# Nine planner constants of a fused attention and feed-forward kernel become a table with sixteen rows

## The chip, the cores and the metric

The kernel runs on one core of a Trainium2 chip. Its time is the device time of one execution in microseconds (us), and lower is better. In the profile the engines have these names: PE is TensorE (matrix products), PEld its loads of weights, DVE is VectorE, ACT is ScalarE, POOL is GpSimd, and SP issues DMA transfers.

## What is computed

One transformer block with adaptive layer norm, for one sequence of 2048 tokens of width 512, in bfloat16:

```python
mod = (silu(c) @ w_mod).reshape(1, 6, 1, 512)
sa, ca, ga, sb, cb, gb = mod[:, 0], ..., mod[:, 5]
h = layernorm(x) * (1 + ca) + sa
x = x + ga * attention(h, wqkv, wo)              # 32 heads of 16
h = layernorm(x) * (1 + cb) + sb
x = x + gb * ((gelu(h @ w_gate) * (h @ w_up)) @ w_down)   # 1792 wide
```

The attention makes 32 x 2048 x 2048 scores and takes the exponential of each of them.

## The kernel before

**Banks and positions.** Scores are made in PSUM, a bank at a time: 128 keys on the partitions and 512 columns, which are 512 queries, or fewer queries and several tiles of keys. All scores together are 2048 such banks, and the kernel puts them into one list, `seq`; the index of a bank in it is its position, `pos`. The queries are cut into seven sets (`SETS`: 512, 512, 256, 256, 256, 128 and 128 tokens). A set takes as many banks as it has tokens, so `ends`, the position at which each set ends, is 512, 1024, 1280, 1536, 1792 and so on. Four neighbouring banks (four heads, the same keys) form a round. The first two units of work, 128 banks, come interleaved; `nsplit` is the position after them.

**Two ways to an exponential.** The score banks of PSUM (`ps_sc`) are six, used as two groups of three (`CH` is 3). Most banks go through ACT: one `ACTIVATE` with the exponential for the two or three banks of a group, written to the ring `E`. Some rounds are done by DVE instead (`new_quad` opens one): for each of the round's four banks one `TENSOR_SCALAR` (`bits`) writes a 16-bit number to `mreg`, `dreg` or `wreg`, and then three operations over 2048 columns (`power_task`: `mant`, `square`, `expo`) make two tiles whose value products PE adds up. A group then has two banks for ACT and one for DVE, or, in the branch of `ALONE`, only banks for DVE. PE multiplies the exponentials by the values into `ps_pv` (`pv_do`); `unit_end` divides by the sum.

**Side work.** Projections, the second layer norm, the output projection and the feed-forward network of the sets that are done run between the scores, piece by piece (`next_side`, `advance`), mostly in the bank `ps_mi`. `plan` gives each of them a start and a due position; `credit` counts the columns of side work that should have been done by now. DVE's work for them and for the rounds lies in `self.tasks`, from which `step` takes it.

**Who sets the order.** The whole order of all engines is fixed while the kernel is built. `rec` notes each operation with what it waits for. `model` keeps a clock for each engine (`self.free`) by formulas for the length of an operation (`cost`), such as, for ACT and DVE,

```python
            return n * 0.833 + (57 if ps else 92)
...
        return n * 1.042 / f + 68
```

with `n` the elements of a partition and `f` a factor for 16-bit operands outside of PSUM. `probe` asks when an operation could begin. The loop in `stream` takes at every turn the time `t` at which PE is free and chooses greedily: the next group of scores, a value product, a piece of side work, or a filler (a product with the identity or with zeros whose result is not used). A filler is put in where PE would wait and the columns of its last 3413 ns, which `short` counts, are below `FILL`; a column counts at full weight for a product over the whole array and at a quarter for one over a part of it. `model` counts a column of PE at 1/2.4 ns throughout. After the loop, `tail` finishes the last two sets with constants of its own (a literal `t + 30` among them), and `prologue`, which lies ahead of the loop, is written out by hand.

**The nine constants.** Each of them is one number for the whole loop before:

- `t + 30` (ready): what can begin within 30 ns counts as ready now.
- `HOLE` 200: the gap in ns on DVE ahead of a bank of scores into which another step is put.
- `BACK` 8: no new round for DVE while this many of its steps wait.
- `FILL` 4200: the columns, as above.
- `credit > 1536` (lag): the credit from which side work goes ahead of scores and value products.
- `+ 500` (early): by how many ns DVE may be busy beyond ACT and still get a bank of the next group.
- `ALONE` 2500: how many ns ACT must be busy ahead for a group to go to DVE alone.
- `AHEAD` 24: how many positions ahead of `pos` a round for DVE must lie, from `nsplit` on.
- `SIDE2` 2500: the credit above which side work gets a second bank, the sixth of the score banks. It is asked only where `pos >= TWO_AT(ends)`, which is `ends[4]`, 1792.

No bank goes to DVE before `("k", 3, 0)`, the last keys of the first heads, is there.

Of the kernel before, what the change touches and what calls it, by code (L numbers as in the profile page):

```python
# [1 line left out]

# [20 lines left out]
NKT = S_TOK // P  # L23
VW = DH + 1
EPS = 1e-5
FILL = 4200


SETS = ((0, 512), (512, 512), (1024, 256), (1280, 256), (1536, 256), (1792, 128), (1920, 128))
# [4 lines left out]
CH = 3  # L34
# [4 lines left out]
CREDIT = 5000  # L39
LATE_AT = lambda ends: ends[4]  # L40
TWO_AT = lambda ends: ends[4]
HOLE = 200
SIDE2 = 2500
ALONE = 2500
AHEAD = 24
NEAR = 8
FIRST = 0
LAST = 3
# [1 line left out]
DUE = lambda ends: (ends[1] + 30, 1420, 1605, ends[4] + 10, ends[5] - 20)  # L50
URGENT = 9
LATE = 2
BACK = 8
END = (0, None)


# [7 lines left out]

COMPUTE = ("pe", "act", "dve", "pool")
ALLENG = ("sp",) + COMPUTE


class _Op:
# [362 lines left out]
class _Kernel(_Recorder):  # L432
# [714 lines left out]
    def short(self, t):  # L1147

        w = 0
        for s, k in reversed(self.log):  # L1150
            if s < t - 3413:
                break
            w += k
        return FILL - w

    def stream(self):
        self.split = True
# [10 lines left out]
        rounds = []  # L1168
        rof = {}
        ends = [0] * len(SETS)  # L1170
# [12 lines left out]
        nsplit = len(seq)  # L1183
# [8 lines left out]
        pos = c = e = rp = loaded = 0  # L1192
# [11 lines left out]
        cand = [k for k, (u, r, g0) in enumerate(rounds) if FIRST <= r < NKT * u[3] // 512 - LAST]  # L1204
# [17 lines left out]

        def new_quad(hot):
            nonlocal quad
            while cand and rounds[cand[0]][2] < pos + (AHEAD if pos >= nsplit else NEAR):
                cand.pop(0)
            if hot or not cand or len(self.spare()) < 2 or pos >= LATE_AT(ends) and self.credit >= CREDIT:
                return False
            rnd = rounds[cand[0]]
            (_, qd, _, W), r, a = rnd  # L1230
            if (a >= pos + 96 or self.backlog() >= BACK or ("v", r * (512 // W) // 4, qd // 2) not in self.have
                    or any(k not in self.have for k in self.keys(seq[a]))):
                return False
            cand.pop(0)
            quad = {"rnd": rnd, "j": [0, 1, 2, 3], "todo": 4, "k": self.spare()[0], "ready": [], "n": 2, "slot": None}
            self.held.add(quad["k"])
            left[rnd[0]] += 1
            self.plain[rnd[0]] -= 1
            vec.update(range(a, a + 4))
            return True  # L1240

        def bits(q, j, k, fill=False):
            kq = self.bufs[q["k"]][0]
            f = lambda: self.ts("dve", kq[:, 512 * j:512 * j + 512].bitcast(U16), self.scp[:, k, :],
                                128 / OCT, BITS_C, ALU.mult, ALU.add)
            if fill and self.free["dve"] + HOLE < self.probe(f):
                self.step("dve", self.free["dve"], 650)
            f()
            q["todo"] -= 1
# [27 lines left out]
        def pv_next():  # L1277

            res = []
            for k in open_rounds():  # L1280
                rnd = rounds[k]
                u, r, g0 = rnd
                if group[u] != cg or any(g0 + j not in self.slot for j in range(4)) or len(res) == 2:
                    break
                if left[u] == 1 and self.blocked(u):
                    break
                src = [self.slot[g0 + j] for j in range(4)]
                if ("v", r * (512 // u[3]) // 4, u[1] // 2) not in self.have:
                    if tq is not None:
                        break  # L1290
                    x = 0.0
                else:
                    x = self.probe(lambda: pv(rnd, 0, src))
                if res:
                    x = max(x, res[0][0])
                res.append((x, 0, k, rnd, 0, src, None))
                if left[u] <= 2:
                    break
            n = 0
            for q in wait:  # L1300
                u = q["rnd"][0]
                if group[u] != cg:
                    break
                for i, src in q["ready"]:
                    if n == 2 or (left[u] == 1 and self.blocked(u)) or (res and left[u] <= 2):
                        break
                    n += 1
                    res.append((self.probe(lambda: pv(q["rnd"], i, src)), 1, i, q["rnd"], i, src, q))
            res.sort(key=lambda x: (max(x[0], t + 30), x[1]))
            return res  # L1310

        def pv_do(x):
# [37 lines left out]

        early, late = self.weight_parts()
        while cg <= group[units[-1]]:
            parts = early or late
            if parts and pos >= loaded and (pos >= ends[FLOW - 1] + 8 if early else ("ffn", FLOW - 1) in self.have):
                parts.pop(0)()
# [3 lines left out]
            t = max(self.pe_now(), virt)  # L1359
# [2 lines left out]

            tq = None
            if c % 2:
                self.two = self.fifth or (pos >= TWO_AT(ends) and self.credit > SIDE2)
            mem, after = take(CH - 1 if (left[units[1]] or self.two) and c % 2 else CH)
            s0 = CH * (c % 2)
            if mem:
                e0 = 0 if e + len(mem) > NSL else e
                if all(owner.get(e0 + i, -1) < rp for i in range(len(mem))):  # L1370
                    tq = self.probe(lambda: self.mm(self.scp[:, s0:s0 + len(mem), 0:P], *filler))
            if tq is not None and tq <= t + 30:
                slack = self.free["act"] - 600 - t
                w = self.next_side()
                if w is not None and pos >= w[1] and self.credit > 1536 and slack > 213 and self.probe(w[4][1]) <= t:
                    self.advance()
                    continue
                if slack > 213 and self.short(t) > 0:
                    self.mm(self.scp[:, s0, :], *filler)
                    continue  # L1380
                if self.free["act"] > t + ALONE and self.free["dve"] < t + 900 and ("k", 3, 0) in self.have:
                    alone = []
                    while len(alone) < CH:
                        if quad is None and not new_quad(overdue()):
                            break
                        alone.append((quad, quad["j"].pop(0)))
                        if not quad["j"]:
                            quad = None
                    if alone:
                        items = [(q["rnd"][2] + j, s0 + i) for i, (q, j) in enumerate(alone)]  # L1390
                        self.require(sorted({k for m, _ in items for k in self.keys(seq[m])}))
                        self.qk([(seq[m], k) for m, k in items])
                        for (q, j), (_, k) in zip(alone, items):
                            bits(q, j, k)
                            close(q)
                        gain(len(items))
                        continue
                g = None
                if len(mem) == CH and ("k", 3, 0) in self.have and self.free["dve"] < max(t + 400, self.free["act"]) + 500:
                    hot = overdue()  # L1400
                    if quad is not None:
                        if not hot - {quad["rnd"][0]}:
                            g = pick(quad)
                    elif new_quad(hot):
                        mem, after = take(CH)
                        g = pick(quad)
                if g is not None:
                    mem, after = take(CH - 1)
# [5 lines left out]
                n = len(mem)  # L1414
# [13 lines left out]
                pos, e, c = after, e0 + n, c + 1  # L1428
                continue
            gap = 1e9 if tq is None else tq - t  # L1430
            tp = pv_next()
            ok = [x[0] <= t + 30 for x in tp[:2]] + [False, False]
            w = self.next_side()
            ts = None
            side = False
            if w is not None and pos >= w[1]:
                ts = self.probe(w[4][1])
                n = w[4][0]
                side = (ts <= t + 30 and (self.credit >= n / 2 or (self.short(t) > 0 and self.credit > -2048))
                        and n / 2.4 <= gap + max(0, self.free["act"] - 600 - t - max(0, gap)))  # L1440
            if ok[0] and (ok[1] or self.pe_mode == 2 or tq is None or not mem) and not (
                    side and self.credit > 1536 and (tq is not None or not mem or self.free["act"] > t + 1200)):
                pv_do(tp[0])
                continue
            if side:
# [2 lines left out]
            if ok[0] and gap > 400:  # L1448
                pv_do(tp[0])
                continue  # L1450
            nxt = [x for x in [tq, ts] + [x[0] for x in tp] if x is not None and x > t + 30]
            if self.tasks:
                nxt.append(max(self.free["dve"], t + 100))
            nxt = min(nxt) if nxt else t + 100
            if gap > 213 and self.short(nxt) > 0:
                fill = next((f for f in fillers() if self.probe(f) <= t + 30), None)
                if fill is not None:
                    fill()
                    continue
# [264 lines left out]
```

## Time and profile before

| what | before |
|---|---|
| median of 3 runs | 834.76 us (834.16 to 834.98) |
| the profiled execution | 833.36 us |
| its span, first to last instruction | 831.6 us |
| ACT busy | 797.4 us, 96% |
| PE busy | 760.6 us, 91% |
| DVE busy | 746.7 us, 90% |
| POOL busy | 4.7 us, 1% |
| DMA | 43.74 MB, mean 53 GB/s |

The profile is of one execution; the times come from other runs. Busy time is the time in which an engine has an instruction at work. The chain that ended last is followed back from the last instruction, at each step to what released it. In the rows of groups stand the line of the program, engine, operation, what is written and read, how often; then busy us, mean ns of one, and the idle time just before them with its releaser. The lines are those of helpers that record all operations: L339 is ACT's, L321 PE's, L343, L351, L356 and L360 are DVE's. A wait "A <- B" is time in which A had to wait for B: us in total, times, the longest. A row of a stretch gives its length, then each engine's busy us with the number of instructions, the granted TensorE clock (1.00 is full speed), the share of the DMA engines and GB/s.

### The profile page before, as it was taken

What the parts mean: (1) busy time and instruction counts of PE and PEld (TensorE: products, weight loads), DVE (VectorE), ACT (ScalarE), POOL (GpSimd) and SP (SyncE); (2) the same over time, 40 slices, a digit from 0 to 9 for tenths busy, and PEclk for the clock granted to TensorE, in tenths of its full rate; (3) what the DMA queues carried; (4) which work ended last, traced back from release to release, by engine and by line L of the source; (5) the groups of instructions that cost most, each with busy time, mean ns of one, the idle gap of its engine ahead of it and who ended that gap; (6) DMA issues with size and microseconds to landing.
All of it is one profiled execution on the core that took longest, in us unless ns stands there. A gap on an engine that the chain in (4) does not pass through costs nothing.

```text
span 831.6 us, 30174 instructions
## 1 busy us (share of the span) xinstructions
PE 760.6 (91%) x13685; PEld 297.1 (36%) x13690; DVE 746.7 (90%) x1335; ACT 797.4 (96%) x743; POOL 4.7 (1%) x13
## 2 busy tenths in 40 slices
PE   7999998989999988899899989999999999999998
PEld 3333332322222222222233333333543344345556
DVE  7857999989999999999899999979999999599874
ACT  6999999999999999999999999999999999999982
POOL 2000000000000000000000000000000000000000
PEclk9999999999999999999999999999999999999999
DMA  8010000000003111110003222112462432500000
GB/s 294 37 28 10 10 10 9 10 9 9 9 5 108 47 46 34 47 34 22 22 8 97 60 60 55 40 29 78 129 173 59 123 99 72 158 11 11 18 9 14
DMA packets 76362, 43.74 MB, mean 53 GB/s; under 512 B 20557, under 2 KB 74634, under 8 KB 76234
## 3 DMA queue, kind: packets, MB, share of 16 engines
q1 hardware_dynamic: 76232, 41.82, 18.0%
q8 instruction: 107, 1.75, 0.9%
q14 instruction: 21, 0.17, 0.1%
q10 hardware_dynamic: 2, 0.00, 0.0%
HBM read 39.18 MB, written 2.61 MB: 50 GB/s over the span
## 4 chain that ended last, share of the span: by engine, by line
ACT 77%; PE 13%; DVE 4%; DMA 3%; SPq 2%; issue 1%; DVEq 0%
ACT E L339 73%; PE ps_sc L321 6%; PE ps_mi L321 5%; ACT hreg L339 3%; SPq L389 2%; ACT L339 2%; PE ps_pv L321 1%; DMA rb<-scr_rec 1%; DVE mreg L351 1%; DMA den<-scr_den 1%; DMA mreg<-in_w_mod_dram 1%; DVE mreg L343 1%; DVE dreg L351 0%; DVE wreg L343 0%; DMA scr_den<-osb 0%
## 5 line engine op out<-in xcount | busy, mean ns | idle before, releaser
L339 ACT ACTIVATE E<-ps_sc 128x1024 bf16<-128x1024 f32 (+1 forms) x705 | 752.9, 1292 | 19.7 <-PE ps_sc L321 19.3
L321 PE MATMUL ps_sc<-qT,kme 32*128 32x256 bf16 (+2 forms) x1600 | 193.2, 304 | 24.3 <-ACT E L339 21.4
L321 PE MATMUL ps_sc<-qT,kmo 32*128 32x256 bf16 (+2 forms) x1664 | 193.2, 298 | 22.3 <-ACT E L339 18.9
L351 DVE TENSOR_SCALAR mreg<-ps_sc 128x512 uint16<-128x512 f32 x256 | 171.9, 685 | 19.6 <-PE ps_sc L321 17.1
L321 PE MATMUL ps_pv<-E,vaug 128*17 128x256 bf16 (+2 forms) x2548 | 150.4, 300 | 1.6 <-DVE osb L360 0.9
L321 PE MATMUL ps_mi<-wreg,mreg 128*32 128x256 bf16 (+1 forms) x1888 | 106.7, 326 | 5.4 <-DVE hreg L343 2.4
L351 DVE TENSOR_SCALAR dreg<-ps_sc 128x512 uint16<-128x512 f32 x148 | 99.9, 685 | 9.5 <-PE ps_sc L321 8.6
L321 PEld LDWEIGHTS ps_sc<-qT,kme 32*128 32x128 bf16 x1600 | 53.3, 92 | 144.1 <-ACT E L339 121.7
L321 PEld LDWEIGHTS ps_sc<-qT,kmo 32*128 32x128 bf16 x1664 | 54.9, 92 | 134.5 <-ACT E L339 117.3
L321 PEld LDWEIGHTS ps_pv<-E,vaug 128*17 128x17 bf16 x2548 | 51.2, 89 | 57.0 <-issue 40.7
L351 DVE TENSOR_SCALAR mreg<-mreg 128x2048 uint16<-128x2048 uint16 x103 | 69.8, 682 | 0.3
L321 PEld LDWEIGHTS ps_mi<-wreg,mreg 128*32 128x32 bf16 x1888 | 41.1, 95 | 46.9 <-issue 18.8
L321 PE MATMUL ps_pv<-mreg,vaug 128*17 128x256 bf16 (+2 forms) x840 | 47.5, 295 | 2.0 <-DVE mreg L343 0.7
L343 DVE TENSOR_TENSOR mreg<-mreg 128x2048 bf16<-128x2048 bf16 x39 | 47.4, 1215 | 0.1
L321 PE MATMUL ps_mi<-hreg,wreg 128*32 128x512 bf16 x480 | 40.3, 385 | 0.6 <-DVE vaug L360 0.5
L321 PE MATMUL ps_mi<-xs,ident 128*32 128x512 bf16 (+1 forms) x432 | 35.0, 380 | 0.1
L321 PE MATMUL ps_mi<-wo,onorm 128*32 128x512 bf16 x416 | 33.7, 384 | 0.5 <-DVE xs L343 0.4
L351 DVE TENSOR_SCALAR dreg<-dreg 128x2048 uint16<-128x2048 uint16 x49 | 33.5, 684 | 0.0
L343 DVE TENSOR_TENSOR hreg<-ps_mi,hreg 128x512 bf16<-128x512 f32 x47 | 32.2, 684 | 1.1 <-PE ps_mi L321 0.7
L360 DVE CAST hreg<-ps_mi 128x512 bf16<-128x512 f32 x46 | 31.5, 685 | 1.7 <-PE ps_mi L321 1.0
L321 PE MATMUL ps_pv<-dreg,vaug 128*17 128x256 bf16 (+2 forms) x464 | 29.1, 303 | 2.1 <-DVE dreg L343 1.3
L343 DVE TENSOR_TENSOR dreg<-mreg,dreg 128x2048 bf16<-128x2048 bf16 x25 | 30.3, 1212 | 0.1
(166 smaller groups left out, 696.4 us busy)
## 6 DMA issues: line engine op xcount, KB each, us to landing
mreg<-in_B_w_up_dram SPq DMA_DIRECT2D x32, 256.0 KB, 2.9
mreg<-in_B_w_gate_dram SPq DMA_DIRECT2D x28, 256.0 KB, 3.5
mreg<-in_B_w_down_dram SPq DMA_DIRECT2D x16, 256.0 KB, 2.8
dreg<-in_B_w_down_dram SPq DMA_DIRECT2D x12, 256.0 KB, 4.8
mreg<-in_w_mod_dram SPq DMA_DIRECT2D x1, 2048.0 KB, 12.8
rb<-scr_rec SPq DMA_DIRECT2D x64, 32.0 KB, 1.8
out_dram<-xs SPq DMA_DIRECT2D x16, 128.0 KB, 2.0
rb<-scr_rec SPq DMA_DIRECT2D x116, 16.0 KB, 1.8
```

The source lines that it names most:

```text
L321: return self.rec("pe", lambda e: e.matmul(out, lhsT, rhs, start=start, stop=stop, tile_position=tp), [lhsT, rhs, *after], [out], cost=(n, ...
L339: return self.rec("act", lambda e: e.activation(out, in_, func, scale=scale, **kw), rd, wr, cost=self.cost("act", out, [in_], "act") + load)
L343: return self.rec(eng, lambda e: e.tensor_tensor(out, a, b, op), [a, b], [out], cost=self.cost(eng, out, [a, b], "tt"))
L351: return self.rec(eng, lambda e: e.tensor_scalar(out, a, s1, s2, **kw), rd, [out], cost=self.cost(eng, out, [a], "ts") + (60 if len(rd) > ...
L360: return self.rec(eng, lambda e: e.tensor_copy(out, in_), [in_], [out], cost=self.cost(eng, out, [in_], "ts"))
L389: return e.dma_start(out, in_)
```

## The change

The five named constants and the four literals become fields of a row of `RULES`. `stream` sets `self.rule` at every turn of its loop by the position, one row for each 128 banks. The rows differ from one another; they were chosen by a hill climb on the time that `model` gives. Nothing else is changed: the operations, their formulas, `plan` with its due positions, `prologue` and `tail` are as before. In the cut diff below, the places where a constant is replaced by the field of the same meaning are shown once each.

```diff
-FILL = 4200
...
-HOLE = 200
-SIDE2 = 2500
-ALONE = 2500
-AHEAD = 24
...
-BACK = 8
+RULES = (
+    (5, 100, 6, 4200, 1024, 400, 3200, 32, 1024),
+    (30, 200, 8, 3600, 1536, 500, 2500, 24, 2500),
+    (30, 200, 8, 4200, 1536, 500, 3200, 28, 2500),
+    (30, 300, 8, 4200, 1536, 400, 1900, 24, 2500),
+    (80, 200, 8, 3600, 2048, 500, 2500, 24, 1800),
+    (15, 200, 8, 4200, 2048, 500, 1900, 24, 3200),
+    (80, 300, 10, 3600, 1536, 650, 2500, 24, 1024),
+    (60, 200, 8, 4200, 1536, 500, 1900, 24, 3200),
+    (30, 200, 8, 4200, 1536, 500, 2500, 24, 3200),
+    (15, 200, 10, 3000, 1536, 500, 2500, 24, 2500),
+    (30, 200, 8, 4200, 1536, 400, 3200, 28, 1024),
+    (30, 200, 8, 4200, 1536, 850, 1900, 32, 1024),
+    (30, 450, 6, 3300, 1536, 500, 1900, 24, 3200),
+    (80, 200, 8, 4200, 2048, 850, 3200, 32, 3200),
+    (30, 300, 10, 4200, 1536, 500, 3200, 28, 2500),
+    (60, 200, 7, 3900, 1536, 850, 2500, 24, 3200),
+)
...
+_Rule = collections.namedtuple("_Rule", "ready hole back fill lag early alone ahead side2")
...
-        return FILL - w
+        return self.rule.fill - w
...
-            while cand and rounds[cand[0]][2] < pos + (AHEAD if pos >= nsplit else NEAR):
+            while cand and rounds[cand[0]][2] < pos + (self.rule.ahead if pos >= nsplit else NEAR):
...
-            if (a >= pos + 96 or self.backlog() >= BACK or ("v", r * (512 // W) // 4, qd // 2) not in self.have
+            if (a >= pos + 96 or self.backlog() >= self.rule.back or ("v", r * (512 // W) // 4, qd // 2) not in self.have
...
-            if fill and self.free["dve"] + HOLE < self.probe(f):
+            if fill and self.free["dve"] + self.rule.hole < self.probe(f):
...
-            res.sort(key=lambda x: (max(x[0], t + 30), x[1]))
+            res.sort(key=lambda x: (max(x[0], t + self.rule.ready), x[1]))
...
         while cg <= group[units[-1]]:
+            self.rule = _Rule(*RULES[min(pos // 128, len(RULES) - 1)])
...
-                self.two = self.fifth or (pos >= TWO_AT(ends) and self.credit > SIDE2)
+                self.two = self.fifth or (pos >= TWO_AT(ends) and self.credit > self.rule.side2)
...
-                if w is not None and pos >= w[1] and self.credit > 1536 and slack > 213 and self.probe(w[4][1]) <= t:
+                if w is not None and pos >= w[1] and self.credit > self.rule.lag and slack > 213 and self.probe(w[4][1]) <= t:
...
-                if self.free["act"] > t + ALONE and self.free["dve"] < t + 900 and ("k", 3, 0) in self.have:
+                if self.free["act"] > t + self.rule.alone and self.free["dve"] < t + 900 and ("k", 3, 0) in self.have:
...
-                if len(mem) == CH and ("k", 3, 0) in self.have and self.free["dve"] < max(t + 400, self.free["act"]) + 500:
+                if len(mem) == CH and ("k", 3, 0) in self.have and self.free["dve"] < max(t + 400, self.free["act"]) + self.rule.early:
```

More of the change, by code (lines that the diff above doesn't have):

```diff
@@ L1 @@
+import collections
 import numpy as np
@@ L1371, in stream @@
                     tq = self.probe(lambda: self.mm(self.scp[:, s0:s0 + len(mem), 0:P], *filler))
-            if tq is not None and tq <= t + 30:
+            if tq is not None and tq <= t + self.rule.ready:
                 slack = self.free["act"] - 600 - t
                 w = self.next_side()
-                if w is not None and pos >= w[1] and self.credit > 1536 and slack > 213 and self.probe(w[4][1]) <= t:
+                if w is not None and pos >= w[1] and self.credit > self.rule.lag and slack > 213 and self.probe(w[4][1]) <= t:
                     self.advance()
@@ L1431, in stream @@
             tp = pv_next()
-            ok = [x[0] <= t + 30 for x in tp[:2]] + [False, False]
+            ok = [x[0] <= t + self.rule.ready for x in tp[:2]] + [False, False]
             w = self.next_side()
@@ L1438, in stream @@
                 n = w[4][0]
-                side = (ts <= t + 30 and (self.credit >= n / 2 or (self.short(t) > 0 and self.credit > -2048))
+                side = (ts <= t + self.rule.ready and (self.credit >= n / 2 or (self.short(t) > 0 and self.credit > -2048))
                         and n / 2.4 <= gap + max(0, self.free["act"] - 600 - t - max(0, gap)))
             if ok[0] and (ok[1] or self.pe_mode == 2 or tq is None or not mem) and not (
-                    side and self.credit > 1536 and (tq is not None or not mem or self.free["act"] > t + 1200)):
+                    side and self.credit > self.rule.lag and (tq is not None or not mem or self.free["act"] > t + 1200)):
                 pv_do(tp[0])
@@ L1450, in stream @@
                 continue
-            nxt = [x for x in [tq, ts] + [x[0] for x in tp] if x is not None and x > t + 30]
+            nxt = [x for x in [tq, ts] + [x[0] for x in tp] if x is not None and x > t + self.rule.ready]
             if self.tasks:
@@ L1455, in stream @@
             if gap > 213 and self.short(nxt) > 0:
-                fill = next((f for f in fillers() if self.probe(f) <= t + 30), None)
+                fill = next((f for f in fillers() if self.probe(f) <= t + self.rule.ready), None)
                 if fill is not None:
```

## The prediction

> **What bounds the kernel now.** I read the first part of the profile's page, then the chain that ended last, then the busy time by stretches, and then the waits.
>
> ```profile
> span 831.6 us, 30174 instructions
> PE 760.6 (91%) x13685; PEld 297.1 (36%) x13690; DVE 746.7 (90%) x1335; ACT 797.4 (96%) x743; POOL 4.7 (1%) x13
> ACT 77%; PE 13%; DVE 4%; DMA 3%; SPq 2%; issue 1%; DVEq 0%
> ```
>
> ACT is busy for 797.4 of 831.6 us and holds 77% of the chain. So 34.2 us of the span are not ACT work. The busy time by stretches shows where they lie:
>
> ```profile
> core 0: us, PE busy (x) PEld busy (x) DVE busy (x) ACT busy (x) POOL busy (x), PEclk, DMA share, GB/s
> 0.00:26.00 26.00, 20.81 (x265) 9.40 (x265) 18.66 (x63) 18.10 (x24) 4.34 (x12) 1.00 0.79 264
> 26.00:78.00 52.00, 47.97 (x868) 17.75 (x860) 36.56 (x87) 51.34 (x48) 0.31 (x1) 1.00 0.05 13
> 78.00:390.00 312.00, 283.02 (x3935) 84.14 (x3935) 301.37 (x482) 311.53 (x288) 0.00 (x0) 1.00 0.10 27
> 390.00:702.00 312.00, 289.74 (x5929) 119.19 (x5926) 294.46 (x518) 309.14 (x278) 0.00 (x0) 1.00 0.27 74
> 702.00:728.00 26.00, 24.31 (x493) 9.60 (x490) 15.53 (x27) 25.77 (x26) 0.00 (x0) 1.00 0.45 127
> 728.00:806.00 78.00, 73.34 (x1966) 40.76 (x1963) 66.80 (x133) 75.28 (x72) 0.00 (x0) 1.00 0.06 13
> 806.00:831.60 25.60, 21.45 (x264) 16.29 (x266) 13.32 (x30) 6.25 (x13) 0.00 (x0) 0.98 0.04 12
> ```
>
> The head (to 26) leaves ACT idle 7.9 us and the tail (from 806) 19.35 us. Between them, in 780 us, ACT is idle for 0.66 + 0.47 + 2.86 + 0.23 + 2.72 = 6.9 us only. There the time is how much work ACT is given. DVE is not full there: from 78 to 806 its idle time is 10.63 + 17.54 + 10.47 + 11.20 = 49.8 us. DVE also does softmax banks, so what the planner moves from ACT to DVE is what can shorten the middle. The waits of these two engines: the first row is ACT's from 26 to 806 us, the second DVE's from 78 to 702, the last two DVE's from 702 to 806 (us in total, times, the longest).
>
> ```profile
> ACT E L339 <- PE ps_sc L321: 6.3, 10, 1.2
> DVE mreg L351 <- PE ps_sc L321: 12.1, 24, 2.3
> DVE dreg L351 <- PE ps_sc L321: 5.7, 9, 2.9
> DVE mreg L351 <- PE ps_sc L321: 4.6, 3, 3.0
> ```
>
> ACT's 6.3 us end on PE's scores. DVE waits for the same thing: it has nothing left but a bank of scores that PE hasn't made, since PE waits for ACT to free a buffer. That is a matter of how early the planner gives DVE its next bank.
>
> **What one moved round is worth.** A round of four banks that DVE takes over leaves ACT, mostly as four groups of three that become groups of two.
>
> ```profile
> L339 ACT ACTIVATE E<-ps_sc 128x1024 bf16<-128x1024 f32 x447 | 441.0, 1146 | 5.9 <-PE ps_sc L321 5.5
> L339 ACT ACTIVATE E<-ps_sc 128x1536 bf16<-128x1536 f32 x250 | 364.4, 1576 | 1.5 <-PE ps_sc L321 1.4
> L351 DVE TENSOR_SCALAR mreg<-ps_sc 128x512 uint16<-128x512 f32 x256 | 171.9, 685 | 19.6 <-PE ps_sc L321 17.1
> L351 DVE TENSOR_SCALAR dreg<-ps_sc 128x512 uint16<-128x512 f32 x148 | 99.9, 685 | 9.5 <-PE ps_sc L321 8.6
> ```
>
> ACT gains 1576 - 1146 = 430 ns a bank, 1.72 us a round. Today 256 + 148 = 404 banks, 101 rounds, go by DVE. A round costs DVE four bank operations and three over the whole round (two bit operations and a multiplication). Their means overlap with their neighbours, so I take the pitch from start to start in a full piece of the timeline:
>
> ```profile
> 202.21 0.69 DVE L351 TENSOR_SCALAR mreg<-mreg 128x2048 uint16<-128x2048 uint16 x1
> 202.81 0.68 DVE L351 TENSOR_SCALAR dreg<-dreg 128x2048 uint16<-128x2048 uint16 x1
> 203.42 0.68 DVE L351 TENSOR_SCALAR mreg<-ps_sc 128x512 uint16<-128x512 f32 x1
> 204.02 1.21 DVE L343 TENSOR_TENSOR mreg<-mreg 128x2048 bf16<-128x2048 bf16 x1
> 205.15 1.28 DVE L351 TENSOR_SCALAR dreg<-ps_sc 128x512 uint16<-128x512 f32 x2
> ```
>
> Six at 0.60 and one at 1.13 make 4.73 us. The round also adds one more set of value products on PE; their cover is PE's wait for ACT (below). If the middle gets shorter by 1.72 us, DVE's idle time falls by that too: each round uses 4.73 + 1.72 = 6.45 us of idle DVE. All 49.8 us would hold 7.7 rounds, 13.3 us: that and ACT's 6.9 us are the ceiling, 20.2 us, of what an order can bring in the middle.
>
> **How far the build's clock can be trusted.** The rows of the table were picked by that clock, so what they bring here hangs on it. It is a sum of formulas in the code, and the trace has the same operations. For ACT it is 0.833 ns an element and 57: 910 ns for two banks, 1336 for three. With the counts above (and the six of one bank at 484) that makes 406.8 + 334.0 + 2.9 = 743.7 us; the trace has
>
> ```profile
> L339 ACT ACTIVATE E<-ps_sc 128x1024 bf16<-128x1024 f32 (+1 forms) x705 | 752.9, 1292 | 19.7 <-PE ps_sc L321 19.3
> ```
>
> 9.2 us more, 13 ns on each. For a bank on DVE it has 512 x 1.042 + 68 = 601 ns, and the pitch above is 0.60. So the clock is 1.2% short on ACT, evenly, and right on DVE. And how many banks each engine gets is fixed at the build: a bank that has moved stays moved, however the waits fall.
>
> **The change, part by part.** No operation of the mathematics is added; constants become rows, one for 128 positions. The 2048 positions run from about 14 us (row below) to 806: a row of the table is some 49 us. 63 of the 144 entries differ from before. Eleven of them can't act: side2 is asked only from position 1792, so it is without effect in rows 0 to 13 (ten entries), and ahead only after position 128 (row 0). Row 8 therefore plans by the old rule.
>
> - early, alone, back, ahead, hole decide when DVE is given a bank. They move both ways: early is 650 or 850 in four rows and 400 in three, alone 1900 in five and 3200 in five, back 10 in three and 6 or 7 in three. That looks like a fit of each stretch, and no general opening. I take half of the ceiling: 24.9 us of idle DVE, 3.9 rounds, 6.6 us. The ends are none (0) and all (13.3). The piece from 702 to 728, where DVE does only 15.53 of 26 us, belongs to row 14 and is where I look first.
> - ready and lag move side work and value products against the scores. Their worth is ACT's wait of 6.9 us in the middle; a quarter, 1.6 us, as the wait is in few places (10 stops). Ends: all of it, and as much again lost.
> - fill (3000 to 3900 in six rows) takes out filler products. The worth is nothing, by these rows:
>
> ```profile
> PEld ps_sc L321 <- ACT E L339: 244.3, 569, 1.2
> L321 PE MATMUL ps_mi<-xs,nil x116: 379/379/390, 135.2 to 728.3; 128*32 128x512 bf16 x116
> ```
>
> PE waits 244.3 us for ACT to free score banks, and that wait covers the fillers; without the cover each would cost up to its 0.38 us.
>
> - side2 in row 15 (3200) gives side work a second bank less often, so some groups stay at three banks. From the rows above, 752.9 less 1650 banks at 0.430 leaves 43.4 us for 703 groups, 0.06 us each: ten groups are 0.6 us, counted as nothing.
>
> Head and tail stay. The chain's first exponentials start at 14.37 us, and what lies before is written out by hand; from 806 us the tail's own loop keeps its constants.
>
> ```profile
> 14.37 26.32 ACT E L339 x23
> PEld ps_mi L321 <- DVE hreg L343: 9.6, 25, 1.0
> ```
>
> Sum: 6.6 + 1.6 = 8.2 us. The profiled execution (span 831.6, 833.36 in all) would come to 825.2; it lies 1.4 below the median of the runs, so for the median 834.76 - 8.2 = 826.5 us.
>
> **Rivals.**
>
> Lost in DVE's lateness: the extra rounds go in, but DVE at 301.37 of 312 us is nearly full, and its copies of sums and projections come later; PE, and then ACT, wait for them. The second row of the last fence is such a wait, 9.6 us in 25 places. If it grows by half, all of that falls on ACT and nothing is won on ACT's own wait, the time is 834.76 - 6.6 + 4.8 = 833.0. Against it: the formula for a bank on DVE fits its pitch, so the plan sees this lateness coming.
>
> The order nearly fills DVE: three quarters of both terms, 10.0 + 5.2 = 15.2, so 819.6.
>
> Slower: the TensorE clock. The filler products go in where PE's recent columns fall below fill, and the build's clock counts a column at 1/2.4 ns always: it has no throttle in it. With fill at 3000 to 3600 in rows 1, 4, 6, 9 and 12, PE may fall below what holds its clock. Rows for it:
>
> ```profile
> 611.90:615.30 3.40, 2.21 (x54) 0.83 (x42) 3.10 (x5) 2.86 (x3) 0.00 (x0) 1.00 0.62 161
> 724.60:728.00 3.40, 2.47 (x52) 0.88 (x44) 2.99 (x6) 3.40 (x5) 0.00 (x0) 1.00 0.11 25
> 827.00:830.40 3.40, 0.73 (x4) 0.12 (x2) 2.14 (x4) 0.00 (x0) 0.00 (x0) 0.99 0.17 57
> 806.00:832.00 26.00, 21.45 (x264) 16.29 (x266) 13.32 (x30) 6.25 (x13) 0.00 (x0) 0.97 0.03 11
> ```
>
> PE kept clock 1.00 through pieces with 2.21 and 2.47 busy of 3.40 us. It lost it only after the piece with 0.73: the mean of the last 26 us is 0.97, which is a loss of 0.8 in the last 1.6 us, about half the clock. The first two pieces bear against the rival: each is as long as the stretch over which the code counts columns (3413 ns), and PE was idle for a third of it without losing clock. One piece at half the clock costs between 2 x 2.21 - 3.40 = 1.0 and (at the middle's 283.02 of 312, 3.08 us) 2.8 us, say 1.9. Five such pieces eat 8.2 us; the five rows hold 5 x 49 / 3.4 = 72. With eight, 15.2 us: 826.5 + 15.2 = about 842.
>
> The Trainium skill (TensorE: Matmul & The Clock Gate, "A second HAM failure mode: psum-queue depth-cycling") tells of this way to lose: a PE that micro-idles between groups while it cycles through PSUM banks swings between half and full clock, without any long gap. By that, thinner filling alone would decide, and the time would be the 842 above. This trace disagrees so far: PE waits 569 times for ACT, up to 1.2 us, and the clock stays at 1.00 in every stretch to 806 us.
>
> That the table does nothing would be the old order, within 1 us of 834.76; 52 acting entries speak against it, and I count it with the first rival.
>
> **How the numbers follow.** A measurement of this kernel tells about 0.2%, 1.7 us, from no change. Forecast (gains of 3.5 to 13): 0.73. Nearly full DVE: 0.06. Lost in lateness or without effect: 0.12, of which 0.05 still gain over 1.7 us, 0.05 lie within it and 0.02 beyond it on the other side. Slower by the clock: 0.09. So faster 0.73 + 0.06 + 0.05 = 0.84, same 0.05, slower 0.11. The range takes in the fuller DVE's 819.6 and goes to a gain of nearly nothing, past the lateness's 833.0: 819.5 to 834.5. What lies outside, 842 above all, has about 0.15.
>
> **What would show it.** Right: more than 404 banks by DVE, some 415 to 425; ACT busy lower by 6 to 7 us from 797.4 while its idle time stays at 32 to 34; DVE idle from 78 us to the tail at 20 to 30 us in place of 49.8, most gained between 696 and 750; clock 1.00 to the tail. Wrong: the same 404 banks and a shorter time, which would mean that waits went and not work; ACT waiting for PE or DVE in the middle above 10 us; a clock below 1.00 in rows 1, 4, 6, 9 or 12, which would make the table a loss; a tail from 806 us that is shorter by more than 2 us, as nothing here moves it.

## The result, and the profile after

The changed kernel takes 827.62 us (median of 6 runs, 826.18 to 828.68) against 834.87 us of the kernel before in the same comparison: ratio 0.9904, 95% interval 0.9883 to 0.9924, so some 8 us faster (7.3 by the medians). The profiled execution took 826.18 us.

The first part of its page and the chain's shares:

```profile
span 824.5 us, 29810 instructions
PE 750.5 (91%) x13502; PEld 293.0 (36%) x13502; DVE 750.9 (91%) x1342; ACT 794.4 (96%) x742; POOL 4.6 (1%) x13
ACT 88%; PE 6%; DVE 3%; DMA 2%; issue 0%; SPq 0%; DVEq 0%
```

The span is 7.1 us shorter. Of that, 3.0 us are less ACT work (797.4 to 794.4), and 4.1 us are less ACT idle time (34.2 to 30.1). The chain runs through ACT for 88% in place of 77%. The busy time by stretches, cut as before but with the tail from 800 us on:

```profile
core 0: us, PE busy (x) PEld busy (x) DVE busy (x) ACT busy (x) POOL busy (x), PEclk, DMA share, GB/s
0.00:26.00 26.00, 21.35 (x254) 9.46 (x258) 18.66 (x63) 17.55 (x23) 4.32 (x12) 1.00 0.80 264
26.00:78.00 52.00, 47.76 (x865) 17.84 (x861) 36.43 (x86) 51.34 (x48) 0.31 (x1) 1.00 0.05 12
78.00:390.00 312.00, 281.41 (x3912) 83.62 (x3911) 302.04 (x483) 311.53 (x288) 0.00 (x0) 1.00 0.11 27
390.00:702.00 312.00, 287.13 (x5863) 118.28 (x5866) 297.68 (x525) 310.44 (x282) 0.00 (x0) 1.00 0.27 74
702.00:728.00 26.00, 25.34 (x498) 9.88 (x498) 22.65 (x42) 26.00 (x26) 0.00 (x0) 1.00 0.46 127
728.00:800.00 72.00, 66.97 (x1880) 38.37 (x1875) 61.70 (x121) 71.84 (x69) 0.00 (x0) 1.00 0.06 14
800.00:824.50 24.50, 20.58 (x257) 15.57 (x254) 11.69 (x25) 5.72 (x11) 0.00 (x0) 1.00 0.04 12
```

ACT's idle time in the middle is now 0.66 + 0.47 + 1.56 + 0 + 0.16 = 2.9 us; it was 6.9. Head and tail together are as before (8.45 + 18.78 against 7.9 + 19.35). From 78 to 390 us ACT was full and is full. DVE's idle time from 78 us to the tail falls from 49.8 to 9.96 + 14.32 + 3.35 + 10.30 = 37.9 us. From 702 to 728 DVE does 22.65 us in place of 15.53, but that is not work taken over from ACT. The first four rows are DVE's busy time from 702 to 728 and from there to the end, before and after; the last four are the score banks that it does from 702 to 728, before and after:

```profile
702.00:728.00 26.00, 15.53 (x27) 1.00 0.45 127
728.00:832.00 104.00, 80.11 (x162) 0.99 0.05 12
702.00:728.00 26.00, 22.65 (x42) 1.00 0.46 127
728.00:832.00 104.00, 73.39 (x146) 1.00 0.05 12
L351 DVE TENSOR_SCALAR dreg<-ps_sc 128x512 uint16<-128x512 f32 x6 | 4.1, 687 | 3.6 <-PE ps_sc L321 3.6
L351 DVE TENSOR_SCALAR mreg<-ps_sc 128x512 uint16<-128x512 f32 x3 | 2.1, 687 | 3.0 <-PE ps_sc L321 3.0
L367 DVE TENSOR_SCALAR dreg<-ps_sc 128x512 uint16<-128x512 f32 x8 | 5.4, 686 | 1.7 <-PE ps_sc L337 1.7
L367 DVE TENSOR_SCALAR mreg<-ps_sc 128x512 uint16<-128x512 f32 x1 | 0.7, 681 | 0.0
```

DVE does nine score banks there in both, and 6.7 us less work behind 728 us; from 702 us to the end it is 95.6 us before and 96.0 after. So it does earlier what it did later. Ahead of 702 us it does 371 banks in place of 365, and behind 728 us 28 in place of 30. The groups of the softmax, ACT's waits from 26 to 800 us, and PE's longest wait over the whole span:

```profile
L355 ACT ACTIVATE E<-ps_sc 128x1024 bf16<-128x1024 f32 x448 | 441.6, 1160 | 2.1 <-PE ps_sc L337 2.0
L355 ACT ACTIVATE E<-ps_sc 128x1536 bf16<-128x1536 f32 x248 | 362.6, 1572 | 1.0 <-PE ps_sc L337 1.0
L367 DVE TENSOR_SCALAR mreg<-ps_sc 128x512 uint16<-128x512 f32 x272 | 182.2, 683 | 12.6 <-PE ps_sc L337 10.1
L367 DVE TENSOR_SCALAR dreg<-ps_sc 128x512 uint16<-128x512 f32 x136 | 91.3, 685 | 7.9 <-PE ps_sc L337 5.9
ACT E L355 <- PE ps_sc L337: 2.4, 5, 0.7
PEld ps_sc L337 <- ACT E L355: 247.1, 576, 1.0
```

DVE does 272 + 136 = 408 banks, 102 rounds: one round more than before, where the prediction had 3.9. ACT's stops for scores in the middle fall from 10 to 5. A stop costs more than its idle time. In the trace of the kernel before, the next operation starts 904 ns (median) after one over two banks where ACT does not stop; the 13 such operations that a gap follows have a mean length of 1111 ns, some 0.2 us more. Five stops fewer fit most of the part of the 3.0 us that one round (1.72 us) leaves open; that part was not measured by itself.

### The profile page after: what moved, and what is told of

Its sections match the earlier page's. It is cut to its first block, busy times and chain, and to the rows that moved or that the text cites. A ratio compares the mean times of both kernels' runs of the same rounds, so it can differ in the third digit from the quotient of the medians.

```text
span 824.5 us, 29810 instructions
## 1 busy us (share of the span) xinstructions
PE 750.5 (91%) x13502; PEld 293.0 (36%) x13502; DVE 750.9 (91%) x1342; ACT 794.4 (96%) x742; POOL 4.6 (1%) x13
## 4 chain that ended last, share of the span: by engine, by line
ACT 88%; PE 6%; DVE 3%; DMA 2%; issue 0%; SPq 0%; DVEq 0%
ACT E L355 84%; PE ps_sc L337 3%; ACT hreg L355 3%; PE ps_mi L337 2%; ACT L355 2%; PE ps_pv L337 1%; DMA rb<-scr_rec 1%; DMA scr_rec<-rden 1%; DVE mreg L367 1%; DMA xs<-in_A_x_dram 0%; SPq L405 0%; DVE hreg L376 0%; DVE wreg L367 0%; DVE onorm L359 0%; DVE wreg L359 0%
## 5 line engine op out<-in xcount | busy, mean ns | idle before, releaser
L355 ACT ACTIVATE E<-ps_sc 128x1024 bf16<-128x1024 f32 (+2 forms) x704 | 749.9, 1298 | 14.5 <-PE ps_sc L337 14.2
L337 PE MATMUL ps_sc<-qT,kme 32*128 32x256 bf16 (+2 forms) x1600 | 193.1, 304 | 25.7 <-ACT E L355 21.8
L367 DVE TENSOR_SCALAR mreg<-ps_sc 128x512 uint16<-128x512 f32 x272 | 182.2, 683 | 12.6 <-PE ps_sc L337 10.1
L337 PE MATMUL ps_mi<-wreg,mreg 128*32 128x256 bf16 (+1 forms) x1920 | 110.2, 326 | 8.0 <-ACT hreg L355 2.4
L367 DVE TENSOR_SCALAR dreg<-ps_sc 128x512 uint16<-128x512 f32 x136 | 91.3, 685 | 7.9 <-PE ps_sc L337 5.9
L337 PE MATMUL ps_pv<-mreg,vaug 128*17 128x256 bf16 (+2 forms) x844 | 49.5, 298 | 3.1 <-DVE mreg L359 2.0
L359 DVE TENSOR_TENSOR mreg<-mreg 128x2048 bf16<-128x2048 bf16 x36 | 43.5, 1207 | 0.1
L359 DVE TENSOR_TENSOR dreg<-mreg,dreg 128x2048 bf16<-128x2048 bf16 x32 | 38.8, 1216 | 0.1
L359 DVE TENSOR_TENSOR mreg<-dreg,mreg 128x2048 bf16<-128x2048 bf16 x28 | 34.0, 1213 | 0.0
L337 PE MATMUL ps_mi<-xs,ident 128*32 128x512 bf16 (+1 forms) x376 | 30.7, 380 | 0.8 <-DVE hreg L359 0.8
L337 PE MATMUL ps_mi<-mreg,hreg 128*32 128x512 bf16 x384 | 31.1, 385 | 0.0
```

Source lines behind the costliest of these rows:

```text
L337: return self.rec("pe", lambda e: e.matmul(out, lhsT, rhs, start=start, stop=stop, tile_position=tp), [lhsT, rhs, *after], [out], cost=(n, ...
L355: return self.rec("act", lambda e: e.activation(out, in_, func, scale=scale, **kw), rd, wr, cost=self.cost("act", out, [in_], "act") + load)
L359: return self.rec(eng, lambda e: e.tensor_tensor(out, a, b, op), [a, b], [out], cost=self.cost(eng, out, [a, b], "tt"))
L367: return self.rec(eng, lambda e: e.tensor_scalar(out, a, s1, s2, **kw), rd, [out], cost=self.cost(eng, out, [a], "ts") + (60 if len(rd) > ...
```

## The experiments

Each kernel was timed in five rounds against the kernel before. Differences in us are the ratio less 1, times 835. "The build's clock" is the end of the plan that `model` gives when the kernel is built: 820.4 for the old constants, 813.5 for the table. In e8, e9 and e10 the new order puts a filler into `ps_mi` between one of the sums in `near_end` and its reciprocal, so those denominators are the filler's; the operations are those of the others, and only their times are used.

**e1 and e2: half of the rows each.**

```diff
-    (rows 0 to 11 of RULES)           # e1; in e2 rows 12 to 15
+    (30, 200, 8, 4200, 1536, 500, 2500, 24, 2500),   # the old constants
```

> Rows 12 to 15 new, rows 0 to 11 with the old nine values. Theory A (each row is good for its stretch): the profiles put 1.2 us of the gain ahead of bank 1536 and 6.0 us behind it, so this keeps 6.0 us: about 828.9. Theory B (the table is one draw that holds only as a whole, and a kernel comes out where the build's own clock puts it): the clock printed at the build ends 1.4 us before that of the old constants (819.0 to 820.4; the whole table 813.5): about 833.5. Theory C (only banks moved to DVE count, 1.7 us a round): 100 rounds against 101 before: about 836.6.

> Rows 0 to 11 new, rows 12 to 15 with the old nine values. Theory A: 1.2 us of the gain: about 833.7. Theory B: the build's clock ends at 817.0, 3.4 us earlier: about 831.5. Theory C: 102 rounds against 101: about 833.2.

e1: 834.57 us, ratio 0.9986 (0.9971 to 1.0001). e2: 833.57 us, ratio 0.9969 (0.9953 to 0.9984). Each row as a help to its own stretch (A) falls for e1: the late rows, behind which the profiles show 6 us of the gain, bring 1.2 us when they start from the order that the old constants left. The two halves make 3.8 us together, and the table 8.0. Rounds alone (C) miss e1, which has one fewer than before and isn't slower. B is within 1 us of both by the ratios.

**e3 and e4: half of the columns each.**

```diff
-    row = RULES[i]
+    row = RULES[i] in early, alone, back, ahead, hole; the old value in the others   # e3; e4 the reverse
```

> The columns early, alone, back, ahead and hole from the table, ready, lag, fill and side2 at their old values. By the prediction's split these columns bring most (6.6 of 8.2 us): about 828.3. Theory B: the build's clock ends at 817.3, 3.1 us earlier: about 831.8. Theory C: 101 rounds as before: no change, 834.9.

> The columns ready, lag, fill and side2 from the table, the other five at their old values. By the prediction's split 1.6 us faster: about 833.3; if the shorter waits seen in the profile after come from these columns, some 5 us: about 830. Theory B: the build's clock ends at 822.8, 2.4 us later than with the old constants: about 837.3, slower than before. Theory C: 100 rounds: about 836.6.

e3: 829.3 us, ratio 0.9931 (0.9905 to 0.9957). e4: 838.49 us, ratio 1.0039 (1.0021 to 1.0057). e4 is slower than before, as B had it and against the prediction's split; by its profile DVE has 100 rounds and ACT works 799.1 us, 1.7 more than before, which is what one round is worth. e3 keeps 5.8 us (4.0 between the spans of the two profiled executions) and has not moved one round. Its DVE groups, the rows of its middle that changed, and ACT's waits in the middle:

```profile
L367 DVE TENSOR_SCALAR mreg<-ps_sc 128x512 uint16<-128x512 f32 x252 | 169.1, 683 | 12.0 <-PE ps_sc L337 10.2
L367 DVE TENSOR_SCALAR dreg<-ps_sc 128x512 uint16<-128x512 f32 x152 | 102.1, 684 | 12.1 <-PE ps_sc L337 10.7
390.00:702.00 312.00, 291.14 (x5971) 120.61 (x5975) 296.69 (x520) 311.51 (x283) 0.00 (x0) 1.00 0.27 75
702.00:728.00 26.00, 23.94 (x487) 9.26 (x482) 22.34 (x37) 26.00 (x28) 0.00 (x0) 1.00 0.46 125
ACT E L355 <- PE ps_sc L337: 2.8, 6, 1.1
```

252 + 152 = 404 banks, as before. So the columns that decide when DVE gets a bank helped here by when, and not by how many: ACT is idle for 0.5 us from 390 to 702 in place of 2.9, and waits 2.8 us for scores in place of 6.3.

**e5 and e6: the old constants with less filling.**

```diff
-FILL = 4200
+FILL = 3000      # e5; 0 in e6
```

> The old constants with fill at 3000 in place of 4200, everywhere; nothing else. The rival of the prediction (the TensorE clock falls where fill is low): clock below 1.00 in stretches of the middle and about 842. Theory B (a kernel comes out where the build's own clock puts it): that clock ends at 815.9 in place of 820.4, so 4.5 us faster than before, about 830.5, with the clock as before.

> The old constants with fill at 0, so that no filler product is made in the loop. Theory B: the build's clock ends at 817.6, 2.8 us earlier, about 832. The clock rival: without any filler the clock must fall in many pieces if fillers matter at all; at 2 us a piece, ten or more of them make it 850 or slower.

e5: 832.52 us, ratio 0.9961 (0.9947 to 0.9975). e6: 854.5 us, ratio 1.0234 (1.0210 to 1.0257). Two places of e5 where the clock fell, each with the piece ahead of it, and five stretches of e6 (columns as above; PEclk is the third number from the end):

```profile
316.30:319.70 3.40, 1.55 (x24) 0.43 (x20) 3.40 (x7) 3.38 (x4) 0.00 (x0) 1.00 0.06 12
319.70:323.10 3.40, 3.39 (x26) 0.63 (x26) 2.58 (x4) 2.81 (x3) 0.00 (x0) 0.50 0.00 0
715.60:719.10 3.50, 2.33 (x53) 0.82 (x44) 1.81 (x4) 3.50 (x5) 0.00 (x0) 0.99 0.92 270
719.10:729.30 10.20, 10.20 (x120) 2.75 (x124) 4.45 (x9) 8.14 (x9) 0.00 (x0) 0.50 0.08 19
```

```profile
0.00:26.00 26.00, 20.23 (x218) 9.36 (x218) 18.67 (x63) 17.66 (x23) 4.32 (x12) 0.87 0.80 264
26.00:78.00 52.00, 45.39 (x737) 16.55 (x729) 34.80 (x84) 48.51 (x45) 0.31 (x1) 0.87 0.05 12
78.00:390.00 312.00, 268.31 (x3571) 78.79 (x3568) 299.13 (x477) 307.10 (x283) 0.00 (x0) 0.95 0.10 27
390.00:702.00 312.00, 282.74 (x5410) 112.13 (x5407) 288.42 (x508) 306.74 (x276) 0.00 (x0) 0.93 0.25 71
728.00:824.00 96.00, 86.04 (x2053) 44.78 (x2048) 73.19 (x145) 89.79 (x87) 0.00 (x0) 0.90 0.12 30
```

The clock rival is real, but it did not decide the table's time. Without filling, the five stretches lose 3.4 + 6.8 + 15.6 + 21.8 + 9.6 = 57 us of clock, which at half speed is some 114 us or 34 pieces of 3.4 us. The kernel is 19.5 us slower than before, so a piece costs on the mean about 0.6 us here (0.65 if the 2.8 us that its clock foresaw are added), where the prediction took 1.9. That ACT goes on from scores already made would explain it, and is not shown. The mean does not hold for every piece: two pieces that can be priced one by one cost 1.3 and 2.0 us (last section). With 3000 everywhere the profile has four such pieces ahead of the tail, and the kernel is still 3.3 us faster; the build's clock has it 4.5 us faster by its order. The profiled execution of the table, which has 3000 to 3900 in six rows, shows 1.00 in every stretch.

**e7, e9 and e10: other draws.**

```diff
-RULES = (sixteen rows)
+RULES = ((5, 100, 10, 3600, 2048, 500, 2500, 24, 3200),) * 16      # e7
+RULES = (the sixteen rows in reversed order)                       # e9
+RULES = ((60, 300, 7, 4200, 1536, 850, 3200, 28, 2500),) * 16      # e10
```

> No table: one row for all positions, (5, 100, 10, 3600, 2048, 500, 2500, 24, 3200), the best by the build's clock of 24 rows whose values were drawn at random (clock 813.0; the 24 lie between 813.0 and 827.0, their mean 820.3). 104 rounds against 101 before. If what counts is a row for each stretch, this has nothing of it and should lie near 835. If the table is one good draw among many, this is as good as the table: about 827.5.

> The new table with its sixteen rows in reversed order: the same rows, none at its place. If each row is a fit of its stretch, misplaced rows are worse than none: slower than before. If the rows are simply better values on the whole, most of the gain stays: about 829. Theory B (a kernel comes out where the build's own clock puts it, and that clock is what was searched): 820.1 against 820.4, 100 rounds by DVE against 101: no change, about 834.6.

> One row for all positions, (60, 300, 7, 4200, 1536, 850, 3200, 28, 2500): the worst by the build's clock of the 24 rows drawn at random (827.0), 98 rounds by DVE against 101. Theory B: 6.6 us slower than before, about 841.5. If the clock's differences between kernels were noise on the chip: near 835.

e7: 827.5 us, ratio 0.9910 (0.9883 to 0.9938). e9: 838.65 us, ratio 1.0029 (1.0006 to 1.0051). e10: 839.7 us, ratio 1.0057 (1.0035 to 1.0078). One row, found as the best of 24 random ones, does what the table does: no stretch needs a rule of its own for this gain. e9 is slower than before, by 2.4 us; that fits misplaced rows, which were to be worse than none, better than B's 0.3 us faster, though its interval begins at 0.5 us. Its profiled execution also lost the clock for one piece, at 318 us, about where the reversed table has the row with fill 3000; that may be a part of it. e9 rules out that the rows are better values on the whole. e7's page and DVE groups show another way to the same time:

```profile
PE 742.9 (90%) x13402; PEld 295.8 (36%) x13402; DVE 756.2 (92%) x1356; ACT 791.8 (96%) x741; POOL 4.6 (1%) x13
L367 DVE TENSOR_SCALAR mreg<-ps_sc 128x512 uint16<-128x512 f32 x272 | 181.6, 686 | 9.6 <-PE ps_sc L337 8.1
L367 DVE TENSOR_SCALAR dreg<-ps_sc 128x512 uint16<-128x512 f32 x144 | 96.0, 685 | 5.3 <-PE ps_sc L337 4.5
ACT E L355 <- PE ps_sc L337: 4.0, 9, 1.0
```

104 rounds, so ACT works 5.6 us less than before, and its stops in the middle are nearly those of before (9 for 10).

**e8: the formula for ACT.**

```diff
-            return n * 0.833 + (57 if ps else 92)
+            return n * 0.833 + (70 if ps else 92)      # with the old constants
```

> The old nine constants; only the formula for an operation on ACT that reads PSUM has 70 ns in place of 57, which is what the trace has more. 104 rounds against 101 before. The build's clock ends at 821.4, of which 700 x 13 ns = 9.1 us are the new formula, so by the old formula 812.3. If the drawn order alone makes the difference: 8 us faster, about 827. If the rules' values are what matters, and these are the old ones: 835.

831.76 us, ratio 0.9955 (0.9938 to 0.9972): 3.8 us faster, half of what B gave. The values of the rules are the old ones, and the order that comes out is faster all the same. What failed is the subtraction in the expectation, which takes 13 ns off for each of 700 operations, as if each one waited for the one before it. With every start of e8's order counted anew with 57 in the formula, the plan ends at 816.8, 3.6 us before that of the old constants; this is a count of the plan alone, and nothing was run for it. By that count B is 0.2 us off. ACT's waits for scores in the middle are longer than before:

```profile
ACT E L355 <- PE ps_sc L337: 7.3, 13, 1.0
```

**e11 and e12: a further climb, and the table beside it.**

```diff
-RULES = (sixteen rows)
+RULES = (e7's row, changed in ready, lag, early, ahead, back and fill for some stretches)   # e11
```

> A new table: the single row of the earlier run that had 104 rounds, climbed on in the build's clock by stretches, fill never below 3600. 105 rounds by DVE against 102 in the table. The build's clock ends at 810.5 (old constants 820.4, the table 813.5). Theory B (a kernel comes out where that clock puts it): 9.9 us faster than before, about 825.5, and 3 us faster than the table. If what is left in the clock is beyond what the chip follows (its waits for transfers and the TensorE clock are not in it): no faster than the table, about 827.6.

> The changed kernel itself, unchanged, on the same chip and in the same rounds as the run beside it: 827.6 by its first six runs, with 2 us from run to run.

e11: 824.28 us, ratio 0.9878 (0.9859 to 0.9898). e12: 826.57 us, ratio 0.9913 (0.9892 to 0.9934). e11 is the fastest of all, by 2.3 us in the medians. Its page, its DVE groups and ACT's waits from 26 us to the tail:

```profile
span 821.6 us, 29657 instructions
PE 741.4 (90%) x13418; PEld 294.6 (36%) x13418; DVE 759.4 (92%) x1363; ACT 790.0 (96%) x738; POOL 4.6 (1%) x13
L367 DVE TENSOR_SCALAR mreg<-ps_sc 128x512 uint16<-128x512 f32 x288 | 192.4, 684 | 8.7 <-PE ps_sc L337 7.2
L367 DVE TENSOR_SCALAR dreg<-ps_sc 128x512 uint16<-128x512 f32 x132 | 87.7, 685 | 3.8 <-PE ps_sc L337 3.3
ACT E L355 <- PE ps_sc L337: 5.0, 9, 1.2
```

105 rounds, four more than before: 6.9 us at 1.72 each, and ACT works 7.4 us less; its wait for scores is 1.3 us shorter (5.0 for 6.3).

**All together**, in us against the kernel before:

| kernel | rounds by DVE | by the build's clock | measured (95%) |
|---|---|---|---|
| the table | 102 | -6.9 | -8.0 (-9.8 to -6.3) |
| e12, the table again | 102 | -6.9 | -7.3 (-9.0 to -5.5) |
| e1, rows 12 to 15 | 100 | -1.4 | -1.2 (-2.4 to 0.1) |
| e2, rows 0 to 11 | 102 | -3.4 | -2.6 (-3.9 to -1.3) |
| e3, columns for DVE | 101 | -3.1 | -5.8 (-7.9 to -3.6) |
| e4, the other columns | 100 | +2.4 | +3.3 (1.8 to 4.8) |
| e5, fill 3000 | 102 | -4.5 | -3.3 (-4.4 to -2.1) |
| e6, fill 0 | 101 | -2.8 | +19.5 (17.5 to 21.5) |
| e7, one row | 104 | -7.4 | -7.5 (-9.8 to -5.2) |
| e8, ACT formula | 104 | -8.1; -3.6 with 57 | -3.8 (-5.2 to -2.3) |
| e9, reversed | 100 | -0.3 | +2.4 (0.5 to 4.2) |
| e10, a bad row | 98 | +6.6 | +4.8 (2.9 to 6.5) |
| e11, climbed again | 105 | -9.9 | -10.2 (-11.8 to -8.5) |

Without e6, where the TensorE clock decides, and e8, where the formula itself was changed, the chip lies on the mean 1.1 us from what the build's clock says. The largest misses are 2.7 us (e3 and e9); for these two and, by 0.1 us, for e10 the build's clock lies outside the interval. Rounds alone, at 1.72 us each, lie on the mean 2.8 us off: they would give e3 nothing and the table 1.7 us.

## Why the prediction was right

**The time.** 826.5 was forecast, 827.62 measured; 8.2 us of gain against 8.0 by the ratio. That it is so close is partly luck. The half of the ceiling and the quarter of the wait stand in no row, and both parts came out otherwise (below).

**The build's clock.** The step that the chip follows this clock held: an order that is shorter by it by 1 us or more is shorter on the chip, e6 apart. In the profiled executions that kept the clock at 1.00 up to the tail, the span is longer than the plan by nearly the same amount: 11.2 us for the kernel before (831.6 to 820.4), 11.0 for the table, 10.3 for e12 and e3, 10.9 for e4, 11.3 for e7 and 11.1 for e11. Only e8, by the new count, is further off, with 13.2. The reason that the prediction gives, 13 ns too few on each operation of ACT, does not hold. In the trace before, where ACT does not stop, an operation over two banks takes 904 ns in the median from start to start (mean 919) and one over three 1331 (mean 1335); the formula has 910 and 1336. Of the 9.2 us, some 4 lie at the 21 stops behind these operations, where the whole length shows, some 4 at operations over two banks with a late start behind them (999 ns or more for 5% of them), and the rest at the small ones.

**The bound.** ACT sets the middle, and head and tail stay: that held (27.2 us of ACT's idle time in both). The place did not: DVE's work grew most from 702 to 728 us, but with nine score banks there as before, and with work that came from behind it.

**The split was wrong.** The term "half of the ceiling, 3.9 rounds, 6.6 us" measured one round, 1.72 us. The term "a quarter of ACT's wait, 1.6 us" measured 4.1 us of idle time in the middle, and about another 1 us fits the stops that are gone. The two errors cancel, and that is luck. The prediction named the sign for this itself (the same banks and a shorter time would mean waits and not work), and it nearly came: 408 banks, where it had 415 to 425. Three more of its signs missed: ACT's work fell by 3.0 us and not by 6 to 7, its idle time went to 30.1 us and not to 32 to 34, and DVE's idle time to 37.9 and not to 20 to 30. It gave each group of constants one effect. e3 shows that early, alone, back, ahead and hole can shorten waits without moving a round, and e4 that ready, lag, fill and side2 from the table are worth less than nothing without them. e11 reaches the forecast split, four rounds and 1.3 us of ACT's waits, with other values: the ceiling was sound, and which part of it a search reaches is a matter of the draw.

**The rivals.** DVE's lateness took nothing that can be seen. The wait that the prediction named for it grew from 9.6 us in 25 places to

```profile
PEld ps_mi L337 <- DVE hreg L359: 11.1, 29, 1.1
```

but ACT's waits in the middle fell. The clock rival did not come for the table, while e6 shows that it exists: the mean clock of an execution is 0.997 to 1.000 in the twelve of the table (e12 with them) and 0.993 to 1.000 in the 73 of the kernel before that stand beside the experiments. The Trainium skill's second way to lose the clock (TensorE: Matmul & The Clock Gate, "A second HAM failure mode: psum-queue depth-cycling") would have it swing where PE often idles briefly between groups. The table's trace disagrees: PE waits for ACT 576 times, and its profiled execution shows 1.00 in every stretch. Where the clock fell in e5 it fell after a piece with 1.55 of 3.40 us busy, and after one with 2.33 of 3.50, which is no emptier than the 2.21 that passed in the kernel before; in e2 it fell after a piece with 3.40 of 3.40 (last section). PE's busy time alone doesn't draw the line, and what does stays open.

## What to carry to other kernels

When a planner's own clock fits the trace by a constant amount, a search in that clock is worth making, and its differences can be expected on the chip to within some 3 us here, 1.1 on the mean. Before reading a meaning into searched values, run a reversed table and the best of some random rows: here one row, the best of 24 by the build's clock, did what sixteen fitted ones did. What the clock leaves out (here the TensorE throttle) has to be held from outside, by a floor under the filling; that kept most of the clock here, not all of it.

## What was not expected of the hardware

The same order loses the TensorE clock in one execution and not in another, and the price depends on the place. e1 has the old values up to row 11, so ACT's first 548 operations are those of the kernel before. In its profiled execution the clock fell in the head, and ACT did 16.09 us of work to 26 us in place of 18.10. The rows are that head, then one piece of it in e1 and in the kernel before:

```profile
0.00:26.00 26.00, 21.09 (x238) 9.79 (x238) 17.69 (x62) 16.09 (x22) 4.33 (x12) 0.93 0.82 264
9.30:12.70 3.40, 3.40 (x30) 2.02 (x29) 0.00 (x0) 0.65 (x1) 0.00 (x0) 0.50 0.97 316
9.30:12.70 3.40, 3.17 (x47) 2.38 (x46) 1.78 (x7) 2.29 (x5) 0.00 (x0) 1.00 1.01 336
```

Behind it each operation of ACT starts 2.0 us later than in the kernel before, and some 2 us later still at 604 us. That piece lies ahead of the first exponentials, in the part that is written out by hand. In the middle, e2 has the table's rows 0 to 11, so ACT's first 547 operations are those of the table. The rows are two pieces of e2 and the second one in the table:

```profile
87.40:90.80 3.40, 3.40 (x64) 1.91 (x65) 3.17 (x7) 3.30 (x4) 0.00 (x0) 1.00 0.11 39
90.80:94.20 3.40, 3.40 (x30) 0.52 (x26) 2.31 (x5) 2.56 (x4) 0.00 (x0) 0.50 0.03 7
90.80:94.20 3.40, 3.40 (x51) 1.17 (x48) 3.17 (x9) 3.40 (x5) 0.00 (x0) 1.00 0.05 17
```

e2 is 1.16 us ahead of the table up to this piece and 0.10 us behind it at 107 us: the piece cost 1.3 us, inside the prediction's 1.0 to 2.8. At 49 us a row it lies in row 1, one of the rows that the prediction named for the rival. A straight line through the 73 executions of the kernel before gives 0.63 us for each 0.001 of mean clock, an estimate of 1.3 us a piece. So the 0.6 us of e6 is a mean for a kernel without filling, and why a piece is cheaper there stays open.
